# Gate and value products of the last block: three of four groups as seven products of halves instead of eight

## The chip, the cores and the metric

The kernel runs on one core of one Trainium2 chip. The metric is device time in microseconds (us) of one execution; the lower the better. TensorE is called PE in the profile, its weight loads PEld, VectorE DVE, ScalarE ACT, GpSimd POOL, and SyncE, which issues most DMAs, SP. Each engine works through its own instructions in order and waits on semaphores for the others.

## The reference

Attention with normalised queries and keys for 8 batches, 12 heads, 448 tokens of width 64, then a gated feed-forward block on the 3,584 x 768 result, everything in float32:

```python
q_n, k_n = rmsnorm(q, g_q), rmsnorm(k, g_k)
attn = softmax(q_n @ k_n.T / 8)
x = (attn @ v)                       # per head; heads joined to 768 columns
g = x @ w_gate                       # 768 x 1536
val = x @ w_val                      # 768 x 1536
out = (g / (1 + exp(-g)) * val) @ w_out   # 1536 x 768
```

## The kernel before

The tokens are cut into four blocks of two batches (2 x 448 tokens). The program is one stream: attention of block 0, then for each block the feed-forward products, between which the attention of the next block is laid. The last block (block 3) has no attention beside it.

**The 15 products.** A matrix product of 2 x 3 by 3 x 3 blocks is done with 15 block products instead of 18. The two rows are the two batches of a block, the 3 x 3 the thirds of the model width and of the hidden width. Each of the 15 products has a left side, a sum of blocks of x (`xs`, held as 128 partitions x 448 tokens, and two of them, since a third of 768 is 2 x 128), and a right side, a sum of weight blocks (made once and kept in DRAM, `up_sides` and `down_sides`). `UP_ORDER` is the order of the 15, and `UP_READ` says to which of six results each is added. A third of the hidden width is 512 columns, four groups g of 128. For a group the six results are six blocks of 128 columns x 448 tokens: three thirds for either batch.

**Gate and value.** `up_product` issues one product: two matmuls of 128 x 128 weights by 448 tokens (L1474), one for each half of the contraction, into one PSUM bank. The products go in turn: gate of side 1, value of side 1, gate of side 2, and so on, 30 for a group and 120 for a block. The gate uses the banks `mm0` and `mm1` in turn, the value the two banks of `at`. After a product ACT copies its bank (6 of 15) or DVE adds it to, or takes it from, a sum (9 of 15, `read`, L1409 to L1415). A bank goes on accumulating along a chain of sides, so a read takes what stands there. When a gate result is whole, ACT makes its silu (L1551), and DVE multiplies it by the value (L1554) into `gt`, the hidden layer.

**Output products.** `down_product` (L1663) does the same for the second matrix product: 15 sides, each for two halves s of the output columns, four matmuls (one for each group) of 448 tokens into bank `mm0` (s = 0) or `mm1` (s = 1). Their left sides are sums over the hidden blocks; the first, side 6, needs results 0 and 1 of every group and lies in `hs`.

**Order.** The program doesn't issue as it is written: each piece of work is given to `Order.add` with its engine, a duration, a due time (`when`), the pieces it comes after, and the buffers it takes from rings of fixed size. `Order.run` lays the pieces out, and the instructions of every engine are issued in that order. `load_sides` brings five sides at a time from DRAM to one of two `ws` buffers over SP.

**Buffers around the change.** `work` holds the natural and turned queries and keys of attention (rings `qk`, `t`, `QT`, `KT`), `es` the exponentials (ring `e`), `st` two double PSUM banks of the scores; in block 3's feed-forward part attention no longer needs them. PSUM has eight banks: `mm0`, `mm1`, two of `at`, four of `st`.

## Time and profile before

| | |
|---|---|
| median of 3 runs | 1456.59 us (1454.47 to 1456.96) |
| span of the profiled execution, first to last instruction | 1452.0 us |
| PE busy | 1426.0 us, 98% |
| DVE, ACT, POOL busy | 879.8, 601.6, 405.7 us |
| gate and value products of block 3 | from 1173.82 to 1354.22 us |
| output products of block 3 | from 1354.22 us on |

The profiled execution is one more execution, whose own time is known as its span of 1452.0 us; the runs are timed from outside, and their median is 4.6 us above it. In the profile a line such as L1474 is a line of the kernel; a name such as `mm<-xs,ws` gives what is written and from what. A float32 matmul is two records of the profile and two weight loads. The ends of matmul records are modelled, so the distance of two starts is the better measure of what a matmul costs. `[0.22 <-PE at L1474]` behind a row is the idle time before it and what ended it.

### The profile page before, as it was taken

To read this page: it belongs to the slowest core of one execution; us is meant where nothing else is said; L and a number is where in the kernel's file an instruction comes from. 1 tells how busy PE (TensorE), PEld (TensorE's weight loads), DVE (VectorE), ACT (ScalarE), POOL (GpSimd) and SP (SyncE) were. 2 spreads that over 40 slices of the span, in tenths; PEclk is the share of its full clock that TensorE was granted. 3 is DMA by queue.
4 is the path that set the end of the run, shared out by engine and by line. 5 is a ranking of instruction groups with operands and counts; after the bars stand their busy time and mean duration, and the time that the engine had idled before them with its cause. 6 is when DMAs were issued, how large, how long until landed. Compare 5 with 4: busy or idle time off the path is not lost.

```text
span 1452.0 us, 19362 instructions
## 1 busy us (share of the span) xinstructions
PE 1426.0 (98%) x6736; PEld 689.5 (47%) x6736; DVE 879.8 (61%) x1485; ACT 601.6 (41%) x1210; POOL 405.7 (28%) x476
## 2 busy tenths in 40 slices
PE   8999999999999999999999999999999999999997
PEld 4455454534444455544444455544444445555553
DVE  5889876878866434546877642455686644442533
ACT  6875444476653222356564122345555322212100
POOL 4756666625443000022443200011434300000000
PEclk9999999999999999999999999999999999999999
DMA  7778979854643533433644623443463452322235
GB/s 196 217 219 268 352 266 310 260 149 90 129 103 64 133 102 92 114 113 70 122 98 86 138 74 107 107 112 93 85 126 77 95 135 73 108 73 90 69 100 110
DMA packets 410416, 193.29 MB, mean 133 GB/s; under 512 B 280004, under 2 KB 390852, under 8 KB 410308
## 3 DMA queue, kind: packets, MB, share of 16 engines
q1 hardware_dynamic: 399040, 190.57, 49.1%
q10 hardware_dynamic: 11140, 1.38, 0.7%
q8 instruction: 55, 0.90, 0.3%
q14 instruction: 53, 0.43, 0.1%
q0 software_dynamic: 128, 0.00, 0.0%
HBM read 157.29 MB, written 34.60 MB: 132 GB/s over the span
## 4 chain that ended last, share of the span: by engine, by line
PE 90%; DMA 3%; DVE 2%; ACT 2%; SPq 1%; issue 1%; POOL 1%; ACTq 0%; DVEq 0%; POOLq 0%
PE at L1474 25%; PE mm L1474 25%; PE mm L1663 23%; PE at L1049 8%; PE st L970 7%; PE st L1080 1%; PE mm L1080 1%; DMA out_dram<-spare 1%; SPq L768 1%; DMA work<-in_k_dram 1%; ACT es L985 1%; DMA xs<-in_moe_w_gate_dram 0%; PE st L908 0%; DMA v<-in_v_dram 0%; ACT work L918 0%
## 5 line engine op out<-in xcount | busy, mean ns | idle before, releaser
L1474 PE MATMUL at<-xs,ws 128*128 128x448 f32 x960 | 401.2, 540 | 2.5 <-DVE v L1413 1.4
L1474 PE MATMUL mm<-xs,ws 128*128 128x448 f32 x960 | 401.7, 541 | 0.2 <-DVE hs L1315 0.2
L1474 PEld LDWEIGHTS at<-xs,ws 128*128 128x128 f32 x960 | 181.4, 190 | 184.7 <-issue 166.7
L1474 PEld LDWEIGHTS mm<-xs,ws 128*128 128x128 f32 x960 | 182.2, 190 | 180.7 <-issue 177.9
L888 POOL TENSOR_TENSOR work<-work,rr 128x448 f32<-128x448 f32 x72 | 71.8, 1016 | 467.5 <-DVE rr L715 341.6
L1663 PE MATMUL mm<-gt,ws 128*128 128x448 f32 x448 | 175.5, 543 | 0.0
L970 PE MATMUL st<-work 64*64 64x448 f32 (+1 forms) x1536 | 151.2, 501 | 10.3 <-ACT work L918 4.9
L985 ACT ACTIVATE es<-st 128x896 f32<-128x896 f32 x129 | 114.2, 914 | 101.6 <-PE at L1049 87.8
L1411 DVE TENSOR_TENSOR gt<-gt,mm 128x448 f32<-128x448 f32 x64 | 39.7, 621 | 188.1 <-PE mm L1474 161.7
L1663 PE MATMUL mm<-hs,ws 128*128 128x448 f32 x384 | 151.3, 544 | 0.0
L990 POOL TENSOR_TENSOR sums<-es 128x896 f32<-128x896 f32 x36 | 77.2, 2145 | 176.8 <-PE st L1080 83.7
L1663 PEld LDWEIGHTS mm<-gt,ws 128*128 128x128 f32 x448 | 83.6, 190 | 83.0 <-issue 80.8
L1551 ACT ACTIVATE st<-gt 128x448 f32<-128x448 f32 x96 | 52.3, 547 | 159.1 <-DVE gt L1415 85.7
L1409 ACT COPY gt<-mm 128x448 f32<-128x448 f32 x80 | 42.6, 532 | 157.5 <-PE mm L1474 157.4
L1049 PE MATMUL at<-es,v 64*64 64x448 f32 (+1 forms) x1032 | 106.0, 507 | 0.0
L1663 PEld LDWEIGHTS mm<-hs,ws 128*128 128x128 f32 x384 | 71.3, 190 | 71.0 <-issue 70.1
L970 PEld LDWEIGHTS st<-work 64*64 64x64 f32 x1536 | 50.9, 133 | 79.1 <-issue 37.4
L1409 ACT COPY v<-at 128x448 f32<-128x448 f32 x96 | 51.0, 532 | 80.4 <-PE at L1474 79.6
L990 POOL TENSOR_TENSOR sums<-sums,es 128x896 f32<-128x896 f32 x36 | 76.0, 2112 | 2.8
L1049 PEld LDWEIGHTS at<-es,v 64*64 64x64 f32 (+1 forms) x1032 | 44.1, 134 | 56.2 <-issue 50.4
L1554 DVE SCALAR_TENSOR_TENSOR gt<-st,v 128x448 f32<-128x448 f32 x96 | 59.7, 622 | 7.3 <-DVE v L1415 0.5
L1411 DVE TENSOR_TENSOR v<-v,at 128x448 f32<-128x448 f32 x64 | 39.8, 621 | 39.6 <-PE at L1474 39.5
(170 smaller groups left out, 1550.5 us busy)
## 6 DMA issues: line engine op xcount, KB each, us to landing
ws<-up_sides SPq DMA_DIRECT2D x32, 1024.0 KB, 5.6
ws<-down_sides SPq DMA_DIRECT2D x16, 1024.0 KB, 5.7
ws<-down_sides SPq DMA_DIRECT2D x28, 512.0 KB, 4.8
ws<-up_sides SPq DMA_DIRECT2D x16, 768.0 KB, 4.9
out_dram<-spare SPq DMA_DIRECT2D x168, 56.0 KB, 2.1
v<-in_v_dram SPq DMA_DIRECT2D x96, 96.0 KB, 2.5
ws<-up_sides SPq DMA_DIRECT2D x32, 256.0 KB, 5.9
ws<-up_sides SPq DMA_DIRECT2D x16, 512.0 KB, 5.8
```

The lines of the kernel that those rows point to most:

```text
L888: nc.gpsimd.tensor_tensor(out=tiles["t", m][:, x], in0=tiles["qk", (m, x)], in1=rr.to_broadcast([P, NC, C]), op=ALU.mult,)
L970: nc.tensor.matmul(st[ds(D * x, D), h, 0:n], tiles["KT", m][rows, ds(P * j + D * of_keys, D)], tiles["QT", m][rows, ds(Q * of_queries, n)] ...
L985: nc.scalar.activation(e, tiles["st", (m, j)][:, :, 0 : S * width(j) // P], AF.Exp)
L990: nc.gpsimd.tensor_tensor(out=to, in0=tiles["e", (m, 0)] if j == 1 else to, in1=e, op=ALU.add)
L1049: nc.tensor.matmul(tiles["at", (m, x)][ds(D * h, D), ds(0, Q) if early else queries], tiles["v", m][rows, j, h], tiles["e", (m, j)][rows, ...
L1080: nc.tensor.matmul(to[ds(D * h + C * x, C)], halves[:, x] if half else many[:, 0:C], term[:, h, 0:Q] if half else term[:, h, ts(x, Q)], st ...
L1409: nc.scalar.copy(to, ps)
L1411: nc.vector.tensor_tensor(out=to, in0=old, in1=ps, op=ALU.add)
L1474: nc.tensor.matmul(ps(), w[:, which, c, at], xs[:, SLOT[x], c], start=fresh and c == 0, stop=c == NC2 - 1, skip_group_check=True,)
L1551: nc.scalar.activation(take(*act, [P, 2, TB])[:, 0, 0:S], to, AF.Silu)
L1554: nc.vector.scalar_tensor_tensor(to, tiles[act][:, 0, 0:S], 1.0 / SCALE, tiles[ready], op0=ALU.mult, op1=ALU.mult,)
L1663: nc.tensor.matmul(banks[s][:, 0:S], w[:, s, g, at], where[x][:, g], start=fresh and g == 0, stop=g == NG - 1, skip_group_check=True,)
```

## The change

In block 3 the four groups of gate and value are no longer done alike (`SEVEN = {3: (1, 2, 3)}`).

1. Group 0 is done in two passes: first its 15 gate products, alone, in `mm0` and `mm1`; at the very end its 15 value products, alone, in the same two banks (`alone`, `pair = 0`).
2. Between the two, groups 1 to 3. For each side, gate and value (two rows of weights), two halves of the contraction and two halves of the tokens make a product of 2 x 2 by 2 x 2 blocks: eight matmuls of 224 tokens. They are done with seven (Winograd's form of Strassen's algorithm), in four streams of banks: X (two matmuls, the two halves of `mm0` or `mm1`), Y (two, a bank of `at`), Z (two, a bank of one `st` tile) and W (one, half a bank of the other `st` tile). Z and W run two sides behind X and Y. The reads are those of `UP_READ`, now for four streams.
3. For that, POOL makes four half-sums of x for each side (`halves_of`, 60 instructions of 128 x 224): S3 over the second half of the tokens of x itself, S2 in `work`, S1 in `hs`, S4 in `es`. After the last group's Y products POOL restores that half of x (`restore`, 15 instructions), which the value pass of group 0 reads.
4. When a result of a group is whole, POOL adds the corners together: one sum on X, three on Y (`plus`, 128 x 224), one on Z (`sow`, 128 x 448; for three results of the last group on DVE); DVE adds W to Y (`top`, 128 x 224); then silu and multiplication, now in SBUF and not in PSUM. The silu of group 0 waits for the end of the seven-product part.
5. The weight sides of the seven products are made ahead, in blocks 1 and 2 (`prepare`, 15 units): a unit loads three sides from `up_sides`, POOL makes four differences of 128 x 384, and SP stores seven sides to `up7` in DRAM. The buffers are `es` and a part of `work`, held until the last unit is done.
6. In the seven-product part, SP loads for every three sides one piece of four weight sides (X, Y; three places) and one of three (Z, W; two places).
7. Output products use the banks in the other order in blocks 0 to 2 (`swapped`), and of the groups in block 3 the sums over group 0 come last (`group_end`).

```diff
-    WS = 10 * NC2 * P
+    WS = 21 * P
 ...
+    SEVEN = {3: (1, 2, 3)}
+    HALF, LAG = S // 2, 2
+    up7 = {
+        g: dram.tile([P, 5, 7, 3, P], F32, name=f"up7_{g}")
+        for g in sorted({g for gs in SEVEN.values() for g in gs})
+    }
 ...
+    SHORT = 40.0
+
+    def up_time(n, g=NG):
+        return sum(SHORT if i in SEVEN.get(n, ()) else 30 * PRODUCT for i in range(g))
 ...
+            b = ("BCDAE".index(CHAIN[x]) % 2 if CHAIN[x] != "E" else 0) ^ flip
 ...
+            pair = 0 if alone else which
+            bank = (pair, b)
 ...
-                        ps(), w[:, which, c, at], xs[:, SLOT[x], c],
+                        ps(), w[:, 0 if alone else which, c, at], xs[:, SLOT[x], c],
 ...
-                "ACT", 0.55, when - 0.5, gate, after=[acc["gate", result]], takes=[act],
+                "ACT", 0.55, when - 0.5, gate, after=[acc["gate", result], seven_done[0]], takes=[act],
 ...
+        places_of = dict(S1=flat_hs, S2=work[:, 2 * NJ * 2 * D * 2 :], S4=flat_es)
 ...
+        def part_of(name, x):
+            tokens = slice(HALF, S) if name in ("A21", "A22", "S3") else slice(0, HALF)
+            if name[0] == "A" or name == "S3":
+                return xs[:, SLOT[x], int(name in ("A12", "A22")), tokens]
+            return places_of[name][:, ts(UP_ORDER.index(x), HALF)]
+
+        def halves_of():
+            for step, x in enumerate(UP_ORDER):
+                before = [old_done[x], *side_done[n, x], down_done.get(n - 1), clusters[EARLY * (n + 1) - 1, "total"]]
+                for i, (to, one, two, op) in enumerate((
+                    ("S3", "A11", "A21", ALU.subtract), ("S2", "A22", "S3", ALU.subtract),
+                    ("S1", "S2", "A11", ALU.add), ("S4", "A12", "S2", ALU.subtract),
+                )):
+                    done = order.add(
+                        "POOL", 0.66, start + (step + 1) * unit + 0.6 * i,
+                        lambda to=to, one=one, two=two, op=op, x=x: nc.gpsimd.tensor_tensor(
+                            out=part_of(to, x), in0=part_of(one, x), in1=part_of(two, x), op=op
+                        ),
+                        after=before, port=True, takes=held if step + i == 0 else [],
+                        uses=held if step + i else [],
+                    )
+                    before = [done]
+                    half_done[x, to] = done
 ...
+        def restore(now):
+            for step, x in enumerate(UP_ORDER):
+                side_done.setdefault((n, x), []).append(
+                    order.add(
+                        "POOL", 0.66, now - 3.0 + step * unit,
+                        lambda x=x: nc.gpsimd.tensor_tensor(
+                            out=part_of("A21", x), in0=part_of("A11", x), in1=part_of("S3", x),
+                            op=ALU.subtract,
+                        ),
+                        after=[third_done[x]], port=True, rank=30.0,
+                    )
+                )
+
+        third_done = {}
+        PARTS = dict(
+            X=((0, "A11"), (3, "S2")), Y=((2, "S1"), (1, "S3")),
+            Z=((0, "A12"), (2, "A22")), W=((1, "S4"),),
+        )
 ...
+        def sevens(begin_seven):
+            nonlocal last
+            q = PRODUCT / 4
+            steps, now = [], begin_seven
+            for k in range(15 * len(seven) + LAG):
+                for stream in "XYZW":
+                    j = k - LAG * (stream in "ZW")
+                    if 0 <= j < 15 * len(seven):
+                        steps.append((now, stream, j // 15, j % 15))
+                        now += q * len(PARTS[stream])
 ...
+                    src = up7[seven[k // 5]][:, k % 5, 4:7] if late else up7[seven[k // 5]][:, k % 5, 0:4]
+                    nc.sync.dma_start(tiles[key], src.rearrange("p w x f -> p (w x f)"))
 ...
+                    for side, (slot, of) in enumerate(PARTS[stream]):
+                        nc.tensor.matmul(
+                            half(ps(), side), w[:, slot, at], part_of(of, x),
+                            start=fresh and side == 0, stop=True, skip_group_check=True,
+                        )
+
+                last = order.add(
+                    "PE", q * n_sides, when, emit,
+                    after=[
+                        load, last, free.get(bank),
+                        *(half_done[x, of] for _, of in PARTS[stream] if of[0] == "S"),
+                    ],
+                    takes=[bank_tile] if opens else [],
+                    uses=[key, *tile_of, *held] + ([bank_tile] if bank_tile and not opens else []), mode="full",
+                )
 ...
+                closing = "DVE" if j == len(seven) - 1 and result in (2, 4, 5) else "POOL"
+                if stream == "X":
+                    ready7["X"] = plus(Xr, Xr, Xl, when + 1.0, [done], [kx])
+                elif stream == "Y":
+                    u4 = plus(Yl, Xr, Yl, when + 1.0, [done, ready7["X"]], [kx, ky])
+                    u3 = plus(Xr, Xr, Yr, when + 1.7, [u4], [kx, ky])
+                    ready7[g, result] = u3, plus(Yr, Yl, Yr, when + 2.4, [u3], [ky])
 ...
+                    def sow(tile_at=tile_at, t=t, g=g, result=result, engine=closing):
+                        to = gt[:, g, result]
+                        eng = nc.gpsimd if engine == "POOL" else nc.vector
+                        eng.tensor_tensor(out=to, in0=to, in1=tile_at("X", t), op=ALU.add)
 ...
+                    def top(tile_at=tile_at, t=t):
+                        to = half(tile_at("Y", t), 0)
+                        of = flat_es[:, 15 * HALF :] if t == "t5" else tile_at("W", t)
+                        nc.vector.tensor_tensor(out=to, in0=to, in1=of, op=ALU.add)
 ...
+                        nc.vector.scalar_tensor_tensor(
+                            to, to, 1.0 / SCALE, tile_at("Y", t), op0=ALU.mult, op1=ALU.mult,
 ...
+                for i, (to, one, two) in enumerate(((2, 1, 0), (3, 5, 2), (1, 5, 1), (6, 4, 3))):
+                    done = order.add(
+                        "POOL", 0.92, when + 8.0 + i,
+                        lambda raw=raw, to=to, one=one, two=two: nc.gpsimd.tensor_tensor(
+                            out=raw[:, to], in0=raw[:, one], in1=raw[:, two], op=ALU.subtract
+                        ),
+                        after=[done], port=True, uses=keys[which],
+                    )
+                up7_done[g, u] = emptied[which] = order.add(
+                    "SP", 0.6, when + 14.0,
+                    lambda raw=raw, g=g, u=u: nc.sync.dma_start(
+                        up7[g][:, u].rearrange("p w x f -> p (w x f)"), raw.rearrange("p w f -> p (w f)")
+                    ),
+                    after=[done], uses=keys[which], moves=[transfer(P, 84 * P)], early=0.0,
+                )
 ...
+        passes = [(g, (0, 1)) for g in range(NG) if g not in seven]
+        if seven:
+            passes[:1] = [(0, (0,)), None, (0, (1,))]
+        users, now = {}, start
+        for one in passes:
+            if one is None:
+                halves_of()
+                begin_seven = now
+                sevens(begin_seven)
+                seven_done[:] = [last]
+                now += SHORT * len(seven)
+                group_end.update({g: now - SHORT * (len(seven) - 1 - i) for i, g in enumerate(seven)})
+                restore(now)
+                continue
 ...
+        swapped[:] = [turn_of[0] ^ 1]
+        bank_of = [s ^ swapped[0] for s in range(2)]
 ...
-                for g in range(NG):
+                for i, g in enumerate(group_end):
                     nc.tensor.matmul(
-                        banks[s][:, 0:S], w[:, s, g, at], where[x][:, g],
-                        start=fresh and g == 0, stop=g == NG - 1, skip_group_check=True,
+                        banks[bank_of[s]][:, 0:S], w[:, s, g, at], where[x][:, g],
+                        start=fresh and i == 0, stop=i == NG - 1, skip_group_check=True,
```

The order of PE around the start of block 3's products, before (lines of the kernel before; L1663 are output products of block 2, L1474 gate into `mm`, value into `at`):

```order
L1663 MATMUL mm0_92<-gt_88,ws_7592 128x448 x4
L1663 MATMUL mm1_93<-gt_88,ws_7592 128x448 x4
L1474 MATMUL mm0_92<-xs_82,ws_7682 128x448 x2
L1474 MATMUL at_94<-xs_82,ws_7682 128x448 x2
L1474 MATMUL mm1_93<-xs_82,ws_7682 128x448 x2
L1474 MATMUL at_94<-xs_82,ws_7682 128x448 x2
```

and after, where the gate pass ends and the seven products start (lines of the changed kernel: L1498 is the former L1474, L1752 the matmuls of 224 tokens):

```order
L1498 MATMUL mm0_95<-xs_82,ws_7914 128x448 x2
L1498 MATMUL mm1_96<-xs_82,ws_7914 128x448 x2
L1752 MATMUL mm0_95<-xs_82,work_80 128x224
L1752 MATMUL mm0_95<-work_80 128x224
L1752 MATMUL at_97<-hs_92,work_80 128x224
L1752 MATMUL at_97<-xs_82,work_80 128x224
L1752 MATMUL mm1_96<-xs_82,work_80 128x224
L1752 MATMUL mm1_96<-work_80 128x224
```

Gate and value no longer alternate; a product of two matmuls of 448 has become four streams of matmuls of 224. In all the block has 60 matmuls of 448 and 315 of 224 where it had 240 of 448.

The order of DVE where a group's results are closed (changed kernel; L1427 to L1431 are reads of banks, L1893 is `top`, L1905 the multiplication, `st` are the banks of Z and W):

```order
L1431 TENSOR_TENSOR gt_91<-st_8006,gt_91 128x448 [waits PE_49]
L1431 TENSOR_TENSOR more_94<-st_8011,more_94 128x224 [waits PE_49]
L1893 TENSOR_TENSOR spare_81<-spare_81 128x224 [waits Pool_49]
L1905 SCALAR_TENSOR_TENSOR gt_91<-gt_91,spare_81 128x448 [waits DVE_49,Activation_49]
L1431 TENSOR_TENSOR gt_91<-st_8006,w0_8383 128x448 [waits PE_49]
L1431 TENSOR_TENSOR spare_81<-st_8011,spare_81 128x224 [waits PE_49]
```

Sums that wait for POOL and multiplications that wait for ACT now stand on DVE between the reads of banks.

The order of SP at the start of block 1 (changed kernel; L1448 loads weight sides for the products, L1941 and L1962 are the loads and the store of `prepare`):

```order
L1448 DMA ws_3946<-up_sides0_83 128x4x512
L1448 DMA ws_3946<-up_sides0_83 128x4x128
L1962 DMA up7_1_88<-es_93 128x2688
L1941 DMA work_80<-up_sides1_84 128x2x384 x2
L1448 DMA ws_3992<-up_sides1_84 128x4x512
L1448 DMA ws_3992<-up_sides1_84 128x4x128
L1962 DMA up7_1_88<-work_80 128x2688
```

Between two loads of weight sides now stands a store, which waits for POOL, and the loads of the next unit; before, the L1448 loads stood one behind the other.

326 lines of the change are left out of this document (285 added, 41 removed).

## The prediction

> **What bounds the kernel now.** I read the page first, then the chain of waits, then busy time by window in the last block, then the timeline at that block's edges.
>
> ```profile
> span 1452.0 us, 19362 instructions
> PE 1426.0 (98%) x6736; PEld 689.5 (47%) x6736; DVE 879.8 (61%) x1485; ACT 601.6 (41%) x1210; POOL 405.7 (28%) x476
> PE at L1474 25%; PE mm L1474 25%; PE mm L1663 23%; PE at L1049 8%; PE st L970 7%; PE st L1080 1%; PE mm L1080 1%; DMA out_dram<-spare 1%; SPq L768 1%; DMA work<-in_k_dram 1%; ACT es L985 1%; DMA xs<-in_moe_w_gate_dram 0%; PE st L908 0%; DMA v<-in_v_dram 0%; ACT work L918 0%
> ```
>
> PE is busy 98% of the span, and half of the chain that ended last is the gate and value products of L1474. Matmul ends are modelled, so the busy share alone proves little; the starts decide. In the last block:
>
> ```profile
> L1474 PE MATMUL mm<-xs,ws 128*128 128x448 f32 x240 | 100.0, 539 | 0.0
> L1474 PE MATMUL at<-xs,ws 128*128 128x448 f32 x240 | 100.0, 539 | 0.0
> ...
> 1173.82 1.67 PE L1474 MATMUL mm<-xs,ws 128*128 128x448 f32 x4
> ...
> 1354.22 12.19 PE L1663 MATMUL mm<-hs,ws 128*128 128x448 f32 x32
> ```
>
> The first product starts at 1173.82, the first output product at 1354.22: 180.4 us for 480 records (two a matmul), with no idle time before any: 0.3758 us a record, though each is drawn 0.54 long. So this stage is exactly its matmuls, and fewer of them shorten the span unless something else becomes late.
>
> ```profile
> core 0: us, PE busy (x) PEld busy (x) DVE busy (x) ACT busy (x) POOL busy (x), PEclk, DMA share, GB/s
> 1309.00:1354.00 45.00, 45.00 (x121) 22.76 (x120) 17.18 (x28) 9.57 (x19) 0.00 (x0) 1.00 0.27 82
> ```
>
> A group takes 45 us; in it DVE works 17.2, ACT 9.6, POOL not at all, at full granted clock (1.00). That is the room the change spends.
>
> **The matmuls.** Removed: groups 1 to 3, 3 x 120 = 360 records x 0.3758 = 135.3 us. Added: 3 x 15 x 7 = 315 matmuls of 224 columns, 630 records. Group 0 keeps its 120 records, 45.1 us, in two passes. What a 224-column record with a full 128 x 128 weight load costs is the term that decides. Today's loads:
>
> ```profile
> 1200.88 1.67 PE L1474 MATMUL mm<-xs,ws 128*128 128x448 f32 x4
> ...
> 1200.88 0.19 PEld L1474 LDWEIGHTS mm<-xs,ws 128*128 128x128 f32 x1 [0.19 <-issue]
> 1201.26 0.19 PEld L1474 LDWEIGHTS mm<-xs,ws 128*128 128x128 f32 x1 [0.19 <-issue]
> ```
>
> A load starts with each record, takes 0.19 and is idle 0.19: it lies beside the matmul ahead of it. Half of 0.3758 is 0.188, so a 224-column record just covers one load. The nearest rows with little moving data:
>
> ```profile
> 10.27 0.56 PE L1756 MATMUL mm<-work,ident 112*128 112x224 f32 x2
> 10.17 0.30 PEld L1756 LDWEIGHTS mm<-work,ident 112*128 112x128 f32 x2
> 15.26 0.96 PE L908 MATMUL st<-ident,work 112*128 112x112 f32 x8
> 15.23 0.78 PEld L908 LDWEIGHTS st<-ident,work 112*128 112x128 f32 x8 [0.75 <-POOL work L881]
> L1756 PE MATMUL mm<-work,ident 112*128 112x224 f32 x2 | 0.6, 360 | 0.0
> L908 PE MATMUL st<-ident,work 112*128 112x112 f32 x96 | 12.0, 265 | 2.1 <-POOL work L881 1.1 <-ACT es L985 0.8 <-ACT more L985 0.2
> L1756 PEld LDWEIGHTS mm<-work,ident 112*128 112x128 f32 x4 | 0.6, 192 | 0.0
> ```
>
> Two 224-column records in 0.56 at 0.36 each start 0.20 apart; their two 0.19 loads fit in 0.30, so they start 0.11 apart: a load need not end before the next begins. Eight transposes of 112 columns in 0.96 start (0.96 - 0.265)/7 = 0.099 apart, against 0.3758 / 4 = 0.094 by columns: 0.005 of fixed cost a record. Bounds a record: 0.188 by columns (118.4 us for 630) and 0.20 by the two-record row (126.0, though that row stands at the start, behind waits). I take 0.190, near the transposes' small surplus, of which part sits in 0.188 already: 119.7 us. The matmuls gain 135.3 - 119.7 = 15.6 us; by the bounds 16.9 and 9.3.
>
> **Who reads them.** Costs of one instruction:
>
> ```profile
> L1411 DVE TENSOR_TENSOR v<-v,at 128x448 f32<-128x448 f32 x16 | 9.9, 622 | 13.2 <-PE at L1474 13.2
> L1409 ACT COPY v<-at 128x448 f32<-128x448 f32 x24 | 12.8, 532 | 23.3 <-PE at L1474 23.3
> L1551 ACT ACTIVATE st<-gt 128x448 f32<-128x448 f32 x24 | 13.1, 548 | 51.3 <-DVE gt L1415 26.5 <-DVE gt L1413 9.8 <-DVE gt L1528 9.5
> L1339 POOL TENSOR_TENSOR spare<-spare 128x128 f32<-128x128 f32 x16 | 7.3, 456 | 0.9
> L1339 POOL TENSOR_TENSOR spare<-spare 128x256 f32<-128x256 f32 x8 | 5.8, 730 | 1.9 <-DVE spare L1315 1.6
> ```
>
> DVE, in the 119.7 us: 111 instructions of 448 columns (81 reads, 9 sums, 18 multiplications, 3 closing sums) at 0.622, 69 us, and 48 of 224, between half and all of 0.622, 15 to 30 us: 84 to 99 us, 70 to 83%. ACT: 54 copies at 0.532, 18 of 224 columns at no more, 18 activations at 0.548: at most 48 us. POOL by its two widths takes 0.456 + 0.00214 us a column beyond 128: 0.66 for 224, 1.14 for 448. It has 60 half-sums, 72 corner sums and 15 restorings of 224 and 15 sums of 448: 147 x 0.66 + 15 x 1.14 = 114 us in the 22.6 us of the gate pass and the 119.7 behind it, 80%. None is the bound, so I cost their work at nothing; PE hides it, and a product bank is wanted again only after two steps of 14 records, 2 x 2.66 us, while a read takes 0.62. The half-sums take 60 x 0.66 = 39.6 us and start with the first gate product; side i is ready at about 2.64 (i + 1), and PE wants it at 22.6 + 2.66 i: 18 us of lead, which stays.
>
> **The seams.** In the two passes of group 0 only two banks alternate: a bank is wanted after one product, not after three.
>
> ```profile
> 1334.68 1.67 PE L1474 MATMUL at<-xs,ws 128*128 128x448 f32 x4
> ...
> 1336.38 0.62 DVE L1411 TENSOR_TENSOR v<-v,at 128x448 f32<-128x448 f32 x1 [0.88 <-PE at L1474]
> ```
>
> This read starts 0.20 behind the product's last record (the next product started at 1336.18) and ends at 0.82 of the 1.50 us that the next one takes. With the load a record (0.38) ahead, 0.3 us are left, less than one other DVE instruction. The gate pass has DVE nearly to itself; the value pass has 9 such reads among about as many multiplications and sums. Between no stall and 9 x 0.32 = 2.9 us I take 1.0, and 0.5 more for the three changes of stream. The output products follow as before: the first needs the sum over results 0 and 1 of group 0, whose last product ends three products (4.5 us) before the pass does, against three DVE instructions of 0.62.
>
> **Loads.** Per three steps (8.0 us) 576 KB and 768 KB replace 1,280 KB per 15 us.
>
> ```profile
> ws<-down_sides SPq DMA_DIRECT2D x28, 512.0 KB, 4.8
> ws<-up_sides SPq DMA_DIRECT2D x16, 768.0 KB, 4.9
> SPq L1428 <- PE at L1474: 425.1, 44, 15.2
> ```
>
> The tighter ring (two pieces, Z and W) has 8.0 us from a piece's last use to the next's first; the load lands in about 4.9. The X and Y load queued behind it on SP has a step more. Covered; were it not, each of 15 pieces would stop PE by what is over. SP can wait: it waits 425 us on these products today.
>
> **Blocks 1 and 2.** 15 units are added: loads (768 KB), four POOL subtractions of 384 columns (1.00 each by the rule above) and a store of 1,344 KB.
>
> ```profile
> 460.00:640.00 180.00, 180.00 (x563) 89.57 (x556) 81.07 (x145) 56.83 (x118) 11.52 (x10) 1.00 0.41 108
> ...
> PE st L1080 <- ACT more L985: 0.8, 2, 0.5
> PE st L970 <- ACT es L985: 0.4, 2, 0.2
> ```
>
> POOL works 11.5 of 180 us there, so 32 us fit. The store waits on SP for POOL; behind it stand the next weight load (slot free 15 us ahead of use) and the next block's queries and keys. From 460 to 1000 us PE waited 1.2 us in all. I cost this at nothing; without that cover a pair of the next block would come late by a product or two, 3.0 us each, once in either block. Swapped output banks: no output product waits today, so nothing.
>
> **The sum.** 180.4 becomes 45.1 + 119.7 + 1.5 = 166.3: 14.1 us less, span 1437.9. The runs' median, 1456.59, is 4.6 above the profiled span; that stays. **1442.5 us.** The best bounds (118.4, no stall) give 1439.7, the worst (126.0 and 2.9 + 0.5) 1450.7.
>
> **Rivals.** *The weight load comes out of hiding* (slower). If the array takes a record only d after its load has ended, and the load starts with the record ahead, a record costs the larger of 0.188 and 0.190 + d; today 0.376 hides any d up to 0.186. It decides from 0.2148 a record on (135.3 / 630): d = 0.025. At d = 0.05 the 630 cost 151, and the time is 1474; at the most, 0.376, it is 1560. Against it speak the two loads 0.11 apart and the eight transposes 0.099 apart, though none of those is this form in a long row. The Trainium skill (TensorE: Matmul & The Clock Gate, Part 3, The mechanism) speaks for it: a weight load overlaps a running matmul only where it targets other rows of the array, and here each uses all 128. By that rule in full today's record would cost about 0.38 + 0.19; the trace has 0.376, so it does not agree.
>
> *POOL falls behind.* POOL and DVE slow each other:
>
> ```profile
> L1528 DVE TENSOR_TENSOR v<-v,v 128x448 f32<-128x448 f32 x3 | 2.5, 843 | 0.1
> ...
> L1528 DVE TENSOR_TENSOR v<-v,v 128x448 f32<-128x448 f32 x4 | 2.5, 624 | 0.1
> ```
>
> The first row is from 130 to 290 us, with POOL busy, the second from the last block, without. At that ratio, 1.35, POOL's 114 us become 154, over the 142.3 it has: 12 us late, 1454. It decides from 1.25 on. DVE, in order, would wait for corner sums ahead of reads, and PE for the banks. Against: only DVE's sums and multiplications with both inputs in SBUF collide, not its reads.
>
> *Blocks 1 and 2 lose what block 3 gains in part*: two products late in either, 12 us, 1454.5; one in either, 1448. That the change doesn't do what it says is out: the order of PE has the 315 short matmuls.
>
> **How the numbers follow.** Forecast (1439.5 to 1446) 0.63; POOL behind (1446 to 1455) 0.15; loads out of hiding 0.08; blocks 1 and 2 (1446 to 1456) 0.06; better than all bounds 0.04; another small loss, to 1453, 0.04. The range 1438 to 1453 leaves out the loads, the worst of POOL and the best, some 0.15. About 0.2% (2.9 us) is what a measurement here can tell: faster means under 1453.7. That holds all but the loads, a little of POOL and of blocks 1 and 2: 0.86; same 0.05; slower 0.09, nearly all the loads.
>
> **What would show it.** Matmuls of 224 columns 0.190 apart (0.20 or more: the loads); PE's idle time before products of the last block under 2 us, and its releaser where more (POOL sums or DVE); POOL near 80% busy through that block and its 224-column instruction near 0.66; the first output product 166 us behind the block's first product; blocks 0 to 2 ending where they did, within 1 us. A short record above 0.21, or POOL's above 0.83, makes the prediction wrong.

## The result, and the profile after

The changed kernel takes 1444.92 us, median of 4 runs (1443.7 to 1448.08), against 1455.53 us for the kernel before beside it (4 runs, 1454.3 to 1456.96). The ratio is 0.9931, 95% interval 0.9915 to 0.9947: 10.6 us faster by the medians, 8 to 12 by the interval. Two later sets of runs gave 0.9933 (0.9913 to 0.9952) and 0.9913 (0.9898 to 0.9928). The forecast was 1442.5, in a range of 1438 to 1453. Two later executions ran at a lower granted clock, one of the change (2733.66 us at 0.80) and one of the kernel with 36 more sums (1515.31 us at 0.93); they are in no ratio and move the two medians below by 0.1 us at most.

The time is near the forecast, but not by the forecast's sum. The page of the changed kernel, its head and busy times:

```profile
span 1446.2 us, 20499 instructions
PE 1412.9 (98%) x7006; PEld 739.1 (51%) x7006; DVE 927.0 (64%) x1566; ACT 612.5 (42%) x1244; POOL 581.1 (40%) x698
```

PE is busy 13 us less, and the span is only 5.8 us shorter than that of before (1452.0). The timeline of PE in block 3, where the gate pass, the seven products, the value pass and the output products (L2076) begin:

```profile
1179.50 1.67 PE L1498 MATMUL mm<-xs,ws 128*128 128x448 f32 x4
...
1202.05 0.54 PE L1752 MATMUL mm<-xs,work 128*128 128x224 f32 x2
...
1323.78 1.67 PE L1498 MATMUL mm<-xs,work 128*128 128x448 f32 x4
...
1346.84 12.19 PE L2076 MATMUL mm<-hs,ws 128*128 128x448 f32 x32
```

From the first gate product to the first output product it is 167.3 us (1346.84 - 1179.50), against 180.4 before: 13.1 us less, where 14.1 were forecast. The rest was lost elsewhere: block 3 began at 1179.50 and not at 1173.82, and from its first output product to the end it took 99.4 us and not 97.8. The same stretches of block 3 by windows:

```profile
core 0: us, PE busy (x) PEld busy (x) DVE busy (x) ACT busy (x) POOL busy (x), PEclk, DMA share, GB/s
1179.50:1202.05 22.55, 22.55 (x61) 11.40 (x60) 9.20 (x15) 3.20 (x6) 20.84 (x32) 1.00 0.50 141
1202.05:1241.00 38.95, 38.79 (x203) 37.77 (x202) 20.33 (x37) 12.94 (x26) 32.20 (x50) 1.00 0.52 182
...
1323.78:1346.84 23.06, 22.79 (x61) 11.32 (x61) 19.64 (x31) 7.28 (x15) 8.95 (x11) 1.00 0.27 75
sum 167.34, PE 166.15 PEld 141.16 DVE 111.22 ACT 51.24 POOL 116.95; mean PE 33.23 PEld 28.23 DVE 22.24 ACT 10.25 POOL 23.39
```

The gate pass takes 22.55 us, its 60 records at 0.3758 with no stall at all, though POOL makes half-sums for 20.8 us of it. The seven products take 121.73 (1202.05 to 1323.78), the value pass 23.06, 0.5 more than 60 records need. POOL is busy 117 us of 167. What PE waited for in block 3, by the list of its waits, and three groups of instructions of POOL and DVE:

```profile
PE st L1752 <- DVE gt L1431: 0.7, 2, 0.3
PE mm L1498 <- POOL sums L1863: 0.3, 1, 0.3
PE at L1752 <- DVE spare L1431: 0.2, 1, 0.2
...
L1863 POOL TENSOR_TENSOR sums<-sums 128x224 f32<-128x224 f32 x8 | 6.7, 832 | 0.4
...
L1905 DVE SCALAR_TENSOR_TENSOR gt<-gt,spare 128x448 f32<-128x448 f32 x10 | 8.5, 862 | 0.5
...
L1427 DVE TENSOR_TENSOR v<-v,mm 128x448 f32<-128x448 f32 x14 | 8.7, 620 | 18.4 <-PE mm L1752 16.3 <-ACT gt L1901 1.9 <-PE mm L1498 0.3
```

DVE's multiplications on two tiles of SBUF (L1905) take 0.862 us beside POOL in place of 0.62. POOL's sums of 224 columns take 0.66 us in the median and 0.832 in the slowest group. DVE's reads of banks (L1427) keep 0.620, so most reads come in time, and PE waits 1.2 us in all.

### The profile page after: what moved, and what is told of

Read it like the earlier page. It is cut to its first block, busy times and chain, and to the rows that moved or that the text cites. A ratio compares the mean times of both kernels' runs of the same rounds, so it can differ in the third digit from the quotient of the medians.

```text
span 1446.2 us, 20499 instructions
## 1 busy us (share of the span) xinstructions
PE 1412.9 (98%) x7006; PEld 739.1 (51%) x7006; DVE 927.0 (64%) x1566; ACT 612.5 (42%) x1244; POOL 581.1 (40%) x698
## 4 chain that ended last, share of the span: by engine, by line
PE 84%; DMA 4%; DVE 4%; SPq 3%; ACT 2%; issue 1%; POOL 1%; ACTq 0%; POOLq 0%; DVEq 0%
PE mm L2076 21%; PE mm L1498 21%; PE at L1498 19%; PE at L1064 7%; PE st L985 7%; PE st L1752 3%; PE at L1752 2%; PE mm L1752 2%; SPq L783 2%; DMA work<-in_k_dram 2%; PE st L1095 1%; PE mm L1095 1%; DMA out_dram<-spare 1%; ACT es L1000 1%; DMA work<-in_q_dram 1%
## 5 line engine op out<-in xcount | busy, mean ns | idle before, releaser
L1498 PE MATMUL mm<-xs,ws 128*128 128x448 f32 x820 | 340.0, 542 | 0.5 <-POOL sums L1863 0.3
L1498 PE MATMUL at<-xs,ws 128*128 128x448 f32 x720 | 301.3, 541 | 4.7 <-DVE v L1429 3.6
L1498 PEld LDWEIGHTS mm<-xs,ws 128*128 128x128 f32 x820 | 155.9, 191 | 154.7 <-issue 150.9
L1498 PEld LDWEIGHTS at<-xs,ws 128*128 128x128 f32 x720 | 135.7, 190 | 142.4 <-issue 124.0
L2076 PE MATMUL mm<-gt,ws 128*128 128x448 f32 x448 | 175.5, 543 | 0.0
L2076 PE MATMUL mm<-hs,ws 128*128 128x448 f32 x384 | 151.4, 545 | 0.0
L2076 PEld LDWEIGHTS mm<-gt,ws 128*128 128x128 f32 x448 | 83.6, 190 | 83.0 <-issue 80.8
L1427 DVE TENSOR_TENSOR gt<-gt,mm 128x448 f32<-128x448 f32 x52 | 32.3, 621 | 134.5 <-PE mm L1498 132.7
L2076 PEld LDWEIGHTS mm<-hs,ws 128*128 128x128 f32 x384 | 71.2, 190 | 71.4 <-issue 69.9
L1575 ACT ACTIVATE st<-gt 128x448 f32<-128x448 f32 x78 | 42.6, 547 | 129.3 <-DVE gt L1431 63.3
L1425 ACT COPY gt<-mm 128x448 f32<-128x448 f32 x65 | 34.6, 532 | 122.8 <-PE mm L1498 122.7
L1955 POOL TENSOR_TENSOR es<-es 128x384 f32<-128x384 f32 x32 | 31.2, 998 | 121.7 <-DMA es<-up_sides 121.1
L1425 ACT COPY v<-at 128x448 f32<-128x448 f32 x74 | 39.4, 532 | 58.2 <-PE at L1498 56.7
L822 ACT ACTIVATE work<-work 128x448 f32<-128x448 f32 (+1 forms) x92 | 52.3, 584 | 22.9 <-DMA work<-in_k_dram 10.3
```

What stands on the lines that cost most here:

```text
L822: nc.scalar.activation(tiles["t", m][:, x], of, AF.Square)
L1425: nc.scalar.copy(to, ps)
L1427: nc.vector.tensor_tensor(out=to, in0=old, in1=ps, op=ALU.add)
L1498: nc.tensor.matmul(ps(), w[:, 0 if alone else which, c, at], xs[:, SLOT[x], c], start=fresh and c == 0, stop=c == NC2 - 1, skip_group_chec ...
L1575: nc.scalar.activation(take(*act, [P, 2, TB])[:, 0, 0:S], to, AF.Silu)
L2076: nc.tensor.matmul(banks[bank_of[s]][:, 0:S], w[:, s, g, at], where[x][:, g], start=fresh and i == 0, stop=i == NG - 1, skip_group_check=True,
```

## Stage by stage, in all the profiles

One table carries most of what follows; the kernels in it are told of below, and two, with more work for POOL, and one with narrower matmuls are left out of it. Each row is one profiled execution; each time is the distance of two starts on PE, read from the timeline as above, and the last column but one goes to the end of the span.

| kernel | before block 0's products | block 0 gate, value | block 0 output | block 1 | block 2 | block 3 gate, value | from block 3's first output product | span |
|---|---|---|---|---|---|---|---|---|
| before | 123.6 | 194.2 | 161.8 | 347.3 | 346.9 | 180.4 | 97.8 | 1452.0 |
| before, again | 123.0 | 197.5 | 162.1 | 347.4 | 346.7 | 180.4 | 97.8 | 1454.9 |
| the change | 124.4 | 196.1 | 163.0 | 348.5 | 347.6 | 167.3 | 99.4 | 1446.2 |
| the change, again | 123.1 | 196.1 | 163.3 | 348.1 | 347.3 | 167.3 | 99.3 | 1444.5 |
| the change, third time | 123.5 | 196.1 | 161.8 | 348.3 | 347.4 | 167.4 | 99.3 | 1443.7 |
| prepare alone | 123.7 | 196.1 | 161.8 | 348.4 | 347.1 | 180.4 | 97.8 | 1455.3 |
| one unit | 123.5 | 196.1 | 163.0 | 347.6 | 347.0 | 167.3 | 97.8 | 1442.3 |
| banks not swapped | 124.2 | 197.6 | 162.9 | 348.2 | 347.3 | 167.4 | 99.4 | 1446.9 |
| prepare paced at 10 | 126.1 | 197.6 | 161.8 | 347.5 | 347.0 | 167.3 | 99.0 | 1446.4 |
| the same, stores in halves | 123.3 | 194.4 | 162.2 | 347.4 | 346.4 | 167.3 | 97.8 | 1438.8 |

## The experiments

**The change again, nothing edited.** Is the loss outside block 3 one execution's?

> The changed kernel, nothing edited. In its first trace block 3 up to its output products is 13.1 us shorter than before, as forecast, but the whole only 5.8 us: block 0 ended 2.7 us later, blocks 1 and 2 together took 3.0 us more, and from block 3's first output product to the end it took 1.6 us more. Theory A (the growth outside block 3 belongs to that one execution, whose time of 1448.1 us was the longest of four): this trace has block 0's output products begin within 1 us of the 317.8 us of before and the end 98 us after block 3's first output product, and the times lie 12 to 14 us under before. Theory B (the change itself costs 2 to 5 us in blocks 0 to 2): 320 and 99 us come again, and the times lie 9 to 11 us under before.

1446.23 us against 1455.27, ratio 0.9933 (0.9913 to 0.9952). Block 3's gain is the same to 0.01 us. Of the 7.3 us lost outside block 3 in the first trace (13.1 - 5.8), 5.6 come again (13.1 - 7.5). The 99.3 and the 9 us are theory B's; the 319.1 at which block 0's output products begin lies between the two theories' figures. But "the change causes it" proved true of a part only, as the next runs show.

**Prepare alone.** Groups 1 to 3 of block 3 stay whole products:

```diff
-    SEVEN = {3: (1, 2, 3)}
+    SEVEN = {}
-        for g in sorted({g for gs in SEVEN.values() for g in gs})
+        for g in (1, 2, 3)
```

> The 15 units are prepared and stored in blocks 1 and 2 as in the change, with the new bank order of the output products, but block 3 runs its four groups in 480 whole products as before, and nobody reads the units. What it costs over before is the price of blocks 1 and 2's additions alone. The prediction (hidden): within 1 us of before, ratio 0.9995 to 1.0005. Theory B (they take from the path; rival 3 in small): 2 to 4 us slower than before, ratio 1.0015 to 1.003, with the gate and value products of block 1 taking 188 us as in the trace of the change against 185.3 before.

1457.08 us against 1455.27, ratio 1.0008 (0.9995 to 1.002). The interval holds both theories; the trace is finer. Blocks 1 and 2 take 348.4 and 347.1 us, 1.1 and 0.3 more than the mean of the two traces of before. And block 0, where nothing is prepared, takes 1.9 more than in the first trace of before: that was the first sign that this trace was itself the odd one.

**One unit.**

```diff
-    PREPARE, ... = {1: [(g, u) for g in (1, 2, 3) for u in range(5)][:8], 2: [...][8:]}, 16.0, {}
+    PREPARE, ... = {1: [(1, 0)]}, 16.0, {}
-    src = up7[seven[k // 5]][:, k % 5, 4:7] if late else up7[seven[k // 5]][:, k % 5, 0:4]
+    src = up7[1][:, 0, 4:7] if late else up7[1][:, 0, 0:4]
 ...
-    after=[*last_load, up7_done[seven[k // 5], k % 5], ...],
+    after=[*last_load, up7_done[1, 0], ...],
```

> Only one unit is prepared, in block 1, and all 15 pieces of the seven products read that one; 14 units, 56 of the subtractions on POOL, 14 loads and 14 stores are left out, so the weights of groups 1 to 3 in block 3 are not the right ones; block 3 does all its work. The prediction (preparing is hidden): within 1 us of the change, 10 to 11 us under before. Theory B: the 2 to 4 us that preparing costs come back, 13 to 14 us under before.

1443.38 us, ratio 0.9914 (0.9897 to 0.9932): 11.9 us under before, between the figures of the two theories, and 2.9 us under the change beside it. Blocks 1 and 2 are back within 0.3 and 0.2 us of before; and the stretch to the end is back at 97.8, which nobody had expected of it.

**Banks not swapped in blocks 0 to 2.**

```diff
-        swapped[:] = [turn_of[0] ^ 1]
+        swapped[:] = [turn_of[0] ^ 1] if seven else [0]
```

> The change without the swap of the output products' banks in blocks 0 to 2 (block 3 keeps its own). The prediction (nothing): within 1 us of the change. Theory C (the swap costs at the seams between output products and the next block's gate products, or gains there): a difference of 1 to 3 us from the change, and the starts of the blocks' stages in the trace move with it at each seam.

1445.82 us, ratio 0.9934 (0.9913 to 0.9955), 0.4 from the change, and its stages lie among those of the change. The swap is nothing, as forecast.

**Before again.** The place in block 0, in the timelines of DVE, POOL and PE of the first trace of before:

```profile
301.60 0.62 DVE L1189 TENSOR_TENSOR hs<-gt,hs 128x448 f32<-128x448 f32 x1
302.14 2.56 DVE L1528 TENSOR_TENSOR gt<-gt,w 128x448 f32<-128x448 f32 x1
...
301.88 2.34 POOL L990 TENSOR_TENSOR sums<-es 128x896 f32<-128x896 f32 x1 [3.72 <-ACT es L985]
304.30 2.35 POOL L990 TENSOR_TENSOR sums<-sums,es 128x896 f32<-128x896 f32 x1
...
305.29 1.77 PE L1474 MATMUL at<-xs,ws 128*128 128x448 f32 x4 [0.38 <-DVE v L1413]
```

The instruction that DVE starts at 301.60, ahead of POOL's first sum, takes its 0.62 us; the next one, behind the sum's start, lasts 2.56, until the sum is done. The second sum meets mostly reads of banks. PE then waits 0.38 for DVE.

> The kernel before, nothing edited, profiled a second time. In the five traces of changed kernels PE waits 2.6 us for VectorE at the end of block 0's gate and value products, where the trace of before has 0.4: there VectorE (tensor_tensor on two tiles of SBUF) stands behind both of POOL's 128x896 sums for 2.5 us each, and in the trace of before behind only one of them, because a slow stretch of 0.35 us on PE let VectorE get one instruction ahead. Theory A (this is a matter of the execution, and the trace of before was a lucky one): the second trace shows two such instructions of 2.5 us, the wait of 2.6 us, block 0's gate and value stage 196.1 us long in place of 194.2, and a time near the median of 1455.3. Theory B (the change causes it): 194.2 us and one such instruction again.

1456.75 us, one run. The same place in its trace, and last the window just behind it, where 0.50 is PE's granted clock:

```profile
301.12 2.54 DVE L1189 TENSOR_TENSOR hs<-gt,hs 128x448 f32<-128x448 f32 x1
303.58 2.49 DVE L1528 TENSOR_TENSOR gt<-gt,w 128x448 f32<-128x448 f32 x1
...
301.05 2.12 POOL L990 TENSOR_TENSOR sums<-es 128x896 f32<-128x896 f32 x1 [3.52 <-ACT es L985]
303.25 2.33 POOL L990 TENSOR_TENSOR sums<-sums,es 128x896 f32<-128x896 f32 x1
...
306.66 2.20 PE L1474 MATMUL at<-xs,ws 128*128 128x448 f32 x4 [2.57 <-DVE v L1413]
...
308.00:311.00 3.00, 3.00 (x6) 1.25 (x4) 2.04 (x4) 2.80 (x4) 0.00 (x0) 0.50 0.21 35
```

Now POOL starts 0.07 us ahead of the instruction that had slipped through: two are held, one behind either sum, and PE waits 2.57 us. The same kernel, so it is a matter of the execution: theory A. The stage took 197.5 us and not the 196.1 of the theory, for another reason: from 307.9 on PE had half its clock for 3.4 us (0.50 in the window above), and there its 448-column records start 0.75 us apart in place of 0.376. Each of the thirteen profiles (those of the table, the two with more work for POOL and the narrower matmuls) has one such stretch in this stage, and four have two. The two causes sort them all: one held instruction and one stretch of half clock, 194.2 and 194.4 us; two and one, 196.1 in seven profiles; two and two, 197.5 to 197.6 in four. Among the seven is the kernel with narrower matmuls, whose program up to block 3 is that of before; among the four is the kernel before itself. So block 0's 1.9 us aren't the change's.

The 1452.0 us of the first trace were some 2 us short of what this kernel mostly does in block 0; the 39 executions of the kernel before beside the later runs have spans of 1450.9 to 1457.9, with a median of 1453.0. The Trainium skill (SBUF — State Buffer, SBUF: two separate sides) says that where a DVE instruction with two SBUF inputs meets a POOL instruction that reads SBUF, whichever starts first has a shared port pair for its whole length and the other is blocked meanwhile; the 2.5 us in place of 0.62 agree, and so do the reads of banks that were not held.

**Widths.** How narrow may a record be before its weight load shows? In the kernel before:

```diff
+                parts = (1, 2, 4, 8)[g] if n == NB - 1 else 1
-                for c in range(NC2):
+                for part in range(parts):
+                    for c in range(NC2):
-                        ps(), w[:, which, c, at], xs[:, SLOT[x], c],
+                            ps()[:, ts(part, S // parts)], w[:, which, c, at],
+                            xs[:, SLOT[x], c, ts(part, S // parts)],
-                        start=fresh and c == 0, ...
+                            start=fresh and c == 0 and part == 0, ...
```

> The kernel before, with block 3's products of groups 0 to 3 cut into 1, 2, 4 and 8 pieces of 448, 224, 112 and 56 columns; the same columns in all, so 120, 240, 480 and 960 records (each with its own weight load) in the four groups. The prediction (columns set the pace, a load hides behind the record before it): 45.1 us for each of the first two groups, at 0.376 and 0.189 us a record. Rival 1 (a load of 0.19 us comes out of hiding under short records): 0.21 us a record or more in group 1, above 50 us. For the narrower pieces, where a load of 0.19 us is longer than its matmul: if the load engine is occupied for 0.19 us by each load, 0.19 us a record, 91 us for group 2 and 182 us for group 3; if the 0.19 us is mostly latency and loads follow one another faster, 0.11 us a record or less, 45 to 53 us for group 2 and 100 us or less for group 3.

1526.0 us, one run. The windows of the four groups (120, 240, 480 and 960 records), then the loads of one tile over all four:

```profile
1175.15:1220.25 45.10, 45.10 (x121) 22.80 (x120) 18.93 (x32) 10.95 (x19) 0.00 (x0) 1.00 0.34 98
1220.25:1265.65 45.40, 45.40 (x241) 45.40 (x240) 17.18 (x28) 9.67 (x18) 0.00 (x0) 1.00 0.27 88
1265.65:1319.24 53.59, 53.59 (x482) 53.59 (x481) 17.17 (x28) 9.67 (x18) 0.00 (x0) 1.00 0.24 75
1319.24:1426.39 107.15, 107.15 (x963) 107.15 (x961) 17.17 (x28) 9.67 (x18) 0.00 (x0) 1.00 0.12 35
...
L1476 PEld LDWEIGHTS at<-xs,ws 128*128 128x128 f32 x900 | 116.9, 192 | 11.2 <-issue 10.6 <-DVE v L1411 0.4 <-DVE v L1413 0.2
```

Per record: 45.40 / 240 = 0.189 us for 224 columns; 53.59 / 480 and 107.15 / 960 are both 0.112, for 112 and for 56 columns. So loads follow one another every 0.112 us, though each is drawn 0.192 long. The 107.15 of group 3 lies just above the 100 that I gave for this case, and far below 182. By an estimate from these rows the load sets the pace below about 133 columns (0.112 / 0.3758 x 448) and the columns above it; that the floor is the load is inferred, since no run made the load narrower. Rival 1 is out: at 224 columns 0.077 us of each record are left over. The Trainium skill (TensorE: Matmul & The Clock Gate, LDWEIGHTS (loading the stationary operand)) gives a load of P columns of weights P / 1.2 ns, by which 128 columns would take an estimated 107 ns: near the 0.112 measured. The transposes (L908 in the kernel before) do not agree with it: they load 128 columns of weights too, on 112 rows, and start 0.096 us apart. The rule of the Trainium skill (TensorE: Matmul & The Clock Gate, Part 3, The mechanism) that a load overlaps only matmuls on other rows does not agree with 0.189 either.

**POOL with more to do** (rival 2), two kernels; the second has 6 for 2. In both, the sums for output product 1, which reuse the place that the added sums write, wait for the last of these:

```diff
+                if stream == "Z":
+                    for extra_i in range(2):
+                        padded[0] = order.add(
+                            "POOL", 0.66, when + 0.5 * extra_i,
+                            lambda: nc.gpsimd.tensor_tensor(
+                                out=flat_hs[:, 15 * HALF :], in0=part_of("A11", 8), in1=part_of("A12", 8), op=ALU.add
+                            ),
+                            after=[last], port=True,
+                        )
 ...
-            combine(1, b2, h0, ..., [..., hs_free[0]], g)
+            combine(1, b2, h0, ..., [..., hs_free[0], padded[0]], g)
```

> The change with 36 more sums of 128x224 on POOL, spread over the products of halves (two for each result that is added up; they write a place that nobody reads). At 0.66 us each they add 24 us to the 88 us that POOL is busy in the 121.7 us of the products of halves. The prediction (POOL has slack there; its work lies beside PE's): within 2 us of the change. Rival 2 (POOL sets the pace, in bursts if not in the mean): up to 24 us slower than the change.

> The change with 108 more sums of 128x224 on POOL over the products of halves, 71 us of work, so that POOL has 88 + 71 + 9 = 168 us to do by the end of the value pass, 144.8 us after the products of halves begin. Both theories have POOL set the end now: 20 to 25 us slower than the change if POOL runs without gaps and its sums keep 0.66 us, more if they take 0.79 to 0.83 as its slower forms did in the trace of the change (30 to 45 us). Less than 10 us would say that POOL's busy time in the profile overstates what it costs.

With 36 more, 1450.76 us, ratio 0.9978 (0.9967 to 0.9988); with 108 more, 1477.24, one run. Windows of the seven products, the value pass and the rest to the end, for the change (its third trace), for 36 (with two rows from the timelines of PE and ACT) and for 108:

```profile
1199.57:1321.30 121.73, 120.81 (x631) 118.44 (x630) 82.31 (x144) 40.72 (x86) 87.10 (x121) 1.00 0.48 170
...
sum 244.13, PE 233.97 PEld 175.17 DVE 145.55 ACT 55.97 POOL 96.05; mean PE 77.99 PEld 58.39 DVE 48.52 ACT 18.66 POOL 32.02
```

```profile
1200.47:1322.37 121.90, 120.95 (x631) 118.46 (x630) 80.78 (x142) 40.62 (x86) 104.59 (x146) 1.00 0.49 170
1322.37:1347.48 25.11, 22.82 (x61) 11.32 (x61) 20.72 (x30) 6.74 (x14) 18.43 (x22) 1.00 0.25 69
...
sum 247.63, PE 234.40 PEld 175.10 DVE 146.46 ACT 55.83 POOL 123.02; mean PE 78.13 PEld 58.37 DVE 48.82 ACT 18.61 POOL 41.01
...
1331.30 0.58 ACT L1911 ACTIVATE gt<-gt 128x448 f32<-128x448 f32 x1 [3.68 <-DVE gt L1891]
...
1332.35 15.30 PE L1499 MATMUL mm<-xs,ws 128*128 128x448 f32 x40 [2.29 <-ACT v L1426]
```

```profile
1200.71:1336.74 136.03, 124.53 (x631) 120.76 (x630) 84.06 (x143) 40.16 (x85) 129.48 (x183) 0.96 0.44 152
1336.74:1368.98 32.24, 24.28 (x61) 11.97 (x61) 18.87 (x27) 7.23 (x14) 31.69 (x43) 0.89 0.19 53
...
sum 274.79, PE 241.87 PEld 178.52 DVE 151.31 ACT 55.87 POOL 172.41; mean PE 80.62 PEld 59.51 DVE 50.44 ACT 18.62 POOL 57.47
```

27 us more on POOL (123.0 - 96.0) cost 3.5 us, nearly all behind the seven products: 2.0 in the value pass and 1.3 from there to the end. It is not the restoring, which is over at 1318.7. In the value pass PE waits 2.29 us for ACT's copy of a bank; ACT, in order, had stood at an activation that waits for a closing sum on DVE (L1891), which ends 8.9 us into the value pass, and 5.1 us into it in the change. 76 us more cost 30.7, at the lower end of the 30 to 45 that were given for slower sums; the added ones took 0.74 us in the mean. Not all of it is POOL's work: behind the waits PE ran at a mean clock of 0.96 and 0.89 in the two windows shown, and its own busy time is 7.9 us longer than in the change (241.9 - 234.0).

So POOL had room for some 24 us at the least (27 - 3.5), and 46 by the second kernel (76 - 30.7), or more by what the clock took. At 86% busy (104.6 of 121.9) it made the seven products only 0.2 us longer. The 3.5 us are more than the 2 that I had for 36, and the runs say more still: 4.5 to 6.5 us by the medians of other sets, 6.5 to 9.5 by the ratios to the kernel before (0.9978 against 0.9933 and 0.9913). All of these are far from the 24 of rival 2.

**Where preparing costs, and what happens at the end.** The last runs are three beside one another.

> The changed kernel, nothing edited, beside the next two. 9 to 10 us under before, and in its trace again 4.8 us from the last packet of the output to the end, where before has 3.1.

```diff
-    ..., 16.0, {}
+    ..., 10.0, {}
```

> The change with the preparing of the units paced at 10 us a unit in place of 16 (the number PREPARE_PACE). Units are prepared in the buffers that the attention of the next block uses; with 8 units at 16 us and some 15 us for the last, they are held until some 145 us into block 1, and PE's order shows one piece of attention and two products displaced at the end of block 1's gate and value products, and one in block 2. At 10 us the order of PE in blocks 0 to 2 is that of before, row for row. Theory A (what preparing costs is this displacement): blocks 1 and 2 take again the 347.3 and 346.8 us that they take before, in place of 348.1 and 347.4, so 1 to 1.5 us under the change. Theory B (it is POOL's or the transfers' company that slows them, wherever they stand): no difference from the change, or slower, since the transfers now come closer together.

```diff
-    lambda ...: nc.sync.dma_start(up7[g][:, u]. ..., raw. ...),
+    lambda ...: [
+        nc.sync.dma_start(up7[g][:, u, i : min(i + 4, 7)]. ..., raw[:, i : min(i + 4, 7)]. ...)
+        for i in (0, 4)
+    ],
```

> The last kernel, with each unit stored by two transfers (four slots and three) in place of one, which makes SP's program 15 issues longer and leaves the work as it is. It asks where the 1.6 us at the very end come from. Theory A (SP's instructions after the last store are fetched from memory in pieces, and the length of SP's program decides whether a piece begins among them; the five traces with 1376 of SP's instructions have 4.7 to 4.9 us from the last packet to the end, the five with 1257 to 1347 have 3.1 to 3.3): the place moves, and 3.1 to 3.3 us come back, 1.5 us under the last kernel, unless the boundary falls among the same few instructions again. Theory B (the seven products' loads or the stores leave something to be cleared up): 4.8 us or more, and no difference in time.

The change: 1444.23 us, ratio 0.9913 (0.9898 to 0.9928). Paced at 10: 1443.65, 0.9910 (0.9894 to 0.9925). With stores in halves: 1441.61, 0.9907 (0.9891 to 0.9922). The ratios' intervals overlap; the stages decide. Blocks 1 and 2 take 347.5 and 347.0, then 347.4 and 346.4 us, in place of 348.3 and 347.4: they are those of before again, theory A. What was displaced: in the change's block 1 the list of waits has one row, and the timeline shows the two waits in it; a piece of attention's scores follows directly on the one before it, where in before a value product stands between the two. The timeline of SP shows the last store of a unit 131 us into the block, which begins at 483.50 (I had worked out some 145):

```profile
PE st L985 <- ACT es L1000: 0.5, 2, 0.3
...
654.07 0.61 PE L985 MATMUL st<-work 64*64 64x224 f32 x8 [0.28 <-ACT es L1000]
654.87 0.98 PE L985 MATMUL st<-work 64*64 64x448 f32 x8 [0.20 <-ACT es L1000]
...
614.49 0.54 SPq L1962 DMA_DIRECT2D up<-work  x1
```

The same displacement, with the same 0.28 and 0.20 us, comes at 1002.6 in block 2. In block 1 one more piece moved ahead of the first two output products, so that gate and value take 3.1 us more and the output products 2.0 less. Paced at 10 the order of PE is that of before, the last store stands 94 us into the block, and the list of waits in block 1's gate and value products is empty, as in before.

The end of the program, in the view of transfers over the last 5 us of before, of the change and of the last kernel (40 slices of 0.126 us; below the second, the queue whose packets are instructions):

```profile
GB/s 134 124 189 104 83 96 126 197 195 165 216 82 21 18 8 64 0 0 0 0 0 64 0 0 0 0 0 64 0 0 0 0 64 0 0 0 0 0 0 0
```

```profile
GB/s 23 70 0 0 0 0 0 0 64 0 0 0 0 0 64 0 0 0 0 0 64 0 0 0 0 0 0 0 0 0 0 0 64 0 0 0 0 0 0 0
...
q14 instruction: 5, 0.04, 3.1%
```

```profile
GB/s 133 126 123 104 85 104 127 202 198 228 150 84 84 9 0 0 0 0 0 0 0 64 0 0 0 0 0 0 0 64 64 0 0 0 0 0 0 0 0 0
```

In before the output's last packets end some 3.1 us ahead of the end, in the change 4.8, with nothing behind them but single packets of instructions (the 64s), the last after a gap of 1.5 us. In the last kernel it is 3.3 again. By the count of SP's instructions: 1257 (before, its second trace and the widths), 1291 (one unit), 1347 (prepare alone) and 1393 (stores in halves) have 3.1 to 3.3 us; 1376 (the change three times, banks not swapped, both POOL kernels) 4.7 to 4.9; 1368 (paced at 10) 4.4. Fifteen issues more end sooner, and the seven products' loads are in both: theory A.

The traces also hold SP's own semaphore instructions, which the views leave out, and these show where the time goes. In each trace with 1376 instructions SP, which steps through its closing instructions every 0.06 to 0.1 us, stands still for 1.4 to 1.6 us ahead of the 1362nd or 1363rd; paced at 10, with 1368, for 1.0 ahead of the 1362nd, which there is another instruction. Programs of 1257 to 1347 don't reach that number, and in the last kernel it falls 12 us before the end, ahead of the closing instructions. So the time is SP's. It isn't the last packet that SP waits for: in the change SP goes on 1.54 us before the end, and that packet comes 0.92 before it. The packet ahead of it, at 2.38, comes within the pause. That SP stands still until such a packet has brought its next instructions is inferred, since the trace doesn't name the engine of a packet.

Not all of this is gained in time. The runs of the last kernel lie 2.2 to 2.3 us above their own spans, those of every other kernel 1.7 to 1.9, so some 0.4 us of what its span loses at the end comes back outside the span; no run here shows why.

The last kernel has the lowest median of all here, though its runs (1441.05 to 1445.53) overlap those of the pace of 10 (1442.85 to 1448.14): block 3 as in the change, and everything outside it as before. Its span, 1438.8, is 13.2 under the first trace of before, which met DVE and POOL in the same lucky way (194.4 and 194.2 us).

## Why the prediction was right, and where not

**"I take 0.190, ... 119.7 us."** The step that carried the forecast held: the median distance of two starts of L1752 is 0.189 us. The bounds were 0.188 and 0.20; the two-record row behind the 0.20 was no price for a long row. The fixed cost of 0.005 a record, read off the transposes, was too large, since modelled ends went into it: their starts lie 0.096 apart and not 0.099, and the 224-column records 0.189 and not 0.188, so it is 0.001 to 0.002.

**Seams, 1.5 us.** Under-sized, and its parts lay elsewhere: the value pass lost 0.5 and not 1.0; the seven products took 121.7 for 630 x 0.189 = 119.1, so 2.6 more, by the distances of starts 1.2 of it at the end of the last group, where PE waits for DVE's reads of the banks of Z and W, 0.4 at either change of group and 0.4 at their begin. Block 3 came to 167.3 and not to 166.3.

**Readers and POOL at nothing.** Nearly right: PE waited 0.9 us for DVE and 0.3 for POOL. POOL did 117 us where 114 were worked out, 70% of the 167 us and not 80% of 142, since the sums of the last results reach into the value pass; the restoring doesn't, it is over at 1320.1, ahead of the pass. The price of 224 columns was 0.70 us in the mean of the 147 and 0.66 in the median; the slowest group, eight sums at 0.832, stands at the 0.83 that was named as a sign against the prediction, and cost 0.3 us. *POOL falls behind* would have needed 24 to 46 us more than it had, by the two kernels with more work. The lead of the half-sums comes to 20 us by the two lines given for it (22.6 - 2.64), and not to 18; no product waited for one.

**Loads out of hiding, 0.08.** Out. The prediction took the 0.19 of the trace as a load's time and so thought a short record just covered it; it covers it with 0.077 us to spare.

**"Blocks 1 and 2 ... I cost this at nothing."** Wrong, by about 1.3 us: 0.8 in block 1 and 0.5 in block 2, as means over the seven profiles with all 15 units paced at 16 (those in the table and the two POOL kernels). I had asked whether POOL and SP have time, and they have. What the sum lacked was the order: the units hold `es` and a part of `work`, the planner places the next block's attention behind their due times, and in PE's own order a value product changed places with a piece of attention in either block. The 0.5 us that PE then waits for ACT is all of block 2's loss and most of block 1's. No product was late by 3.0 us, as rival 3 had it; with the pace at 10 it costs nothing that the traces show.

**The end.** The prediction let everything behind block 3's first output product stand; it became 1.5 us longer, through a pause of SP among its last instructions, and no view that I read would have told it.

**"The runs' median ... is 4.6 above the profiled span; that stays."** Wrong, and it hid the losses. The runs of these kernels lie some 1.8 us above their own spans (1448.08 and 1446.2, 1456.75 and 1454.9). The rest was the first trace of before, an execution with a short block 0. So the span forecast, 1437.9, was missed by 8.3 us in the first trace: 1.0 in block 3, 5.7 ahead of it, and 1.5 behind it. Of the 5.7, 1.8 lie in blocks 1 and 2, and 3.9 up to the end of block 0 (0.9 before its products, 1.9 in gate and value, 1.2 in output). The 1.9 are settled above. The rest is of the size by which executions of one kernel differ: the end of block 0 lies at 479.6 and 482.6 in the two traces of before, at 481.2 with the narrower matmuls, and at 481.3 to 483.5 in the three of the change. Whether some of it is the change's is not shown. The 2.8 us too much in the offset took a part of it back.

So there is luck in how near the time came. By the runs the gain was 10.6 us and not the 14.1 of the sum; 1.1 of the 3.5 between them didn't show, since the kernel before took 1455.53 us beside the change and not the 1456.59 from which the forecast was taken.

**Blocks 0 to 2 "ending where they did, within 1 us"** was therefore a poor test: two traces of the same kernel begin block 3 at 1173.82 and 1176.69.

The mechanism held: 13.1 of the 14.1 us forecast for block 3 came in each of the profiles with the seven products and no added sums, less about 3 us that I had at nothing, and nothing of rivals 1 and 2.

## What to carry to other kernels

Where PE's starts stand at the pace of the columns and nothing waits, fewer columns are time saved, here 13.6 us (135.3 - 121.7) of the 16.9 that the columns alone would give, as long as the records stay wide enough for their loads; measure that width, since a load's bar in the trace is longer than the distance at which loads can follow one another. Work that is put beside it for nothing still holds buffers, and a planner answers with another order: compare the order of the engine that bounds, stage by stage, and free such buffers early. Profile the kernel before twice before losses of 2 us are charged to a change, and look at the clock of each stage in both.

## What the runs showed of the hardware that was not expected

- A float32 record with a full 128 x 128 weight load takes 0.112 us at the least, at 112 as at 56 columns; at 224 it takes 0.189, at 448 0.376. A transpose of 112 columns, with a load of 112 rows, takes 0.096.
- Whether DVE's instruction on two SBUF tiles starts 0.07 us behind POOL's sum of 896 columns or ahead of it decides 1.9 us of block 0 (one or two instructions of 2.5 us; 194.2 against 196.1). A stretch of 3.4 us at half of PE's clock, one in nine profiles and two in four, decides 1.4 more.
- The program's end depends on its length: 1.6 us more between the last packet of the output and the end at 1376 instructions of SP than at 1257, 1347 or 1393, and SP pauses for 1.4 to 1.6 us at the 1362nd or 1363rd.
